# Probabilities turned on VectorE, a later landing in the order, other care for VectorE, and an untied end, in a fused attention and expert kernel

## The chip, the cores and the metric

One core of one Trainium2 chip. The time is the device time of one execution in microseconds (us), the median of several. Beside it stands one profiled execution, from which all rows below are read. Engines: TensorE (PE, matmuls), VectorE (DVE), ScalarE (ACT), GpSimd (POOL), SyncE (SP, here only an issuer of DMA transfers). Each takes its own queue of instructions in order.

## What is computed

```python
q_s = softmax(q, axis=-1); k_s = softmax(k, axis=2)          # 4 x 8 heads, 576 x 64 each
x = q_s @ (k_s.T @ v)                                        # to 2304 tokens x 512
h = x @ w_in                                                 # 512 -> 2048
g = where(h >= 1, h, where(h <= -1, 0, (h + 1)**2 / 4))
x = g @ w_out                                                # 2048 -> 512
p = domain_probs / (domain_probs.sum(-1) + 1e-9)             # 2304 x 4
out = sum(p[:, e] * (relu(x @ w1[e]) @ w2[e]) for e in range(4))   # 512 -> 1024 -> 512
```

Inputs are normal random numbers; the first layer's weights come in double precision, the rest in single.

## The kernel before

The 2304 tokens are cut into five blocks of 512, 512, 512, 256 and 512 (block 0 to 4). `PASSES` puts blocks 1 and 0 into a first pass and blocks 2 and 4, with block 3 as `rest`, into a second. In each pass all first-layer weights are used (kind "a"), then the weights of the four experts (kind "b"). Within a kind the hidden width is taken in chunks of 128 and the chunks in groups, one after the other over the blocks. Every product is made of three matmuls of rounded halves (`products`, L1114 to L1116). Except in the first pass's first layer, a pair of blocks and a pair of chunks are multiplied with seven products in place of eight (`strassen`); in the second pass's experts the second matrix too (`second_pairs`), so that there the pair's results are transposed outputs that have to be combined and turned at the end (`finish_pairs`: `total`, then `turned`), while block 3's come out in rows (`finish_expert`, then a store to `out`).

Around the matmuls the other engines prepare: a weight is loaded into `words`, rounded to its high half by a cast (L479, ScalarE or VectorE) and subtracted for its low half (L484, VectorE or GpSimd). `strassen` needs sums of quarters of the weights (`sums`, also L484). In the first pass's experts these are made once and stored to DRAM (`keep_sums`); in the second they are loaded. First-layer weights are converted once and `kept` in DRAM. Attention of the last two batches (`keys`, `queries`) runs beside the first pass's experts.

No engine's order is written out by hand. `Order.run` plays the kernel forward in Python while it is built: each piece of work is a generator that yields an engine with a duration, a list of engines with durations to choose from, an event, or a number, which is its due time in steps of the order. Among the work that can start earliest, the lowest due time goes first. The instructions are emitted in that order, so durations and due times that the planner holds decide each queue's order; at run time the engines wait on semaphores. Three of its rules matter here:

- `arrival` says when a transfer lands: 128 partitions' bytes at 360 GB/s behind the transfer before, plus a constant of 0.9 us.
- `way` chooses between engines. It takes the earliest end, where an engine's duration is lengthened by its recent load (half-life 40 us), a weight of 6 for VectorE, 1 for ScalarE and 0 for GpSimd, and `order.care`:

```python
weight = 0.0 if isinstance(t.want, Soon) else self.WEIGHT[own] * self.care
end = start + d * (1 + weight * self.busy(own, self.now) / self.SPAN)
```

- `order.care` is 1.0 until the second pass's experts begin, then 0.1 (set in `ups`).

`norm_probs` loads the probabilities into `pn` (128 partitions x 18 token tiles x 4 experts), normalises them on VectorE and stores those of blocks 2 and 4 to DRAM as four rows of 1024 (`rows_of_p`), turned by the store's access pattern. In the second pass's experts `load_p` loads each row, broadcast over all partitions, and `weighted` multiplies with it. `downs` emits the second matrix's matmuls group by group: for each group it yields its due step, the weight, the hidden values, and a PSUM bank of `out_banks`. The last group's order is: `second_pairs` of blocks 2 and 4, then block 3's plain matmuls, then, at due time `len(steps)`, the totals, the transposes and the stores.

Of the kernel before, what the change touches and what calls it, by code (L numbers as in the profile page):

```python
# [17 lines left out]
P = 128  # L18
# [46 lines left out]
class Order:  # L65
# [4 lines left out]


    HOP = 0.2
    SPAN = 40.0
    WEIGHT = {DVE: 6.0, ACT: 1.0, POOL: 0.0, PE: 0.0, SP: 0.0}
    NEAR = 0.05
# [77 lines left out]
    def arrival(self, issued, size):  # L153

        self.dma_free = max(issued + 0.45, self.dma_free) + size * P / 360e3
        return self.dma_free + 0.9

    def rank(self, t, engine):
        return t.due - self.AHEAD.get((t.kind, engine), 0)
# [22 lines left out]
def dve(n):  # L182
    return DVE, 0.14 + n * 0.00107
# [15 lines left out]
def attention_moe_kernel(  # L199
# [46 lines left out]
    LAST = 2  # L246
    LATER = 4
    CARE = 0.1
    GATE_DUE = 1
    groups = []  # L250
    for pair, rest in PASSES:
# [45 lines left out]
    one = const.tile([P, 1], F32, name="one")  # L297
    rebias = const.tile([P, 1], F32, name="rebias")
    pn = const.tile([P, NT // P, NE], F32, name="pn")
    psum_p = const.tile([P, NT // P], F32, name="psum_p")  # L300


# [202 lines left out]
    def norm_probs():  # L505
        start = Event()
        start.set(150.0)
        yield start
        for i in range(NT // P):
            for o, n, rows in token_rows(probs, i * P, P):  # L510
                t = yield SP, 0.65
                nc.sync.dma_start(out=pn[o:o + n, i, :], in_=rows)
        late = Event()
        late.set(t + 3)
        yield late
        t = yield dve(300)
        nc.vector.tensor_reduce(out=psum_p, in_=pn, axis=AX.X, op=ALU.add)
        nc.vector.tensor_scalar(out=psum_p, in0=psum_p, scalar1=EPS, scalar2=None, op0=ALU.add)
        nc.vector.reciprocal(out=psum_p, in_=psum_p)
        nc.vector.tensor_tensor(  # L520
            out=pn, in0=pn, in1=psum_p.unsqueeze(2).to_broadcast([P, NT // P, NE]), op=ALU.mult
        )
        probs_in.set(t)
        i0 = blocks[PASSES[1][0][0]][0] // P
        at = 0
        for bi in PASSES[1][0]:
            b0, n = blocks[bi]
            for i in range(n // P):
                t = yield SP, 0.65
                nc.sync.dma_start(  # L530
                    out=rows_of_p[:, at:at + P].rearrange("e p -> p e"), in_=pn[:, b0 // P + i, :]
                )
                at += P
        rows_in.set(t + 5)


# [700 lines left out]
    def ups():  # L1237
        for s, (g, j) in enumerate(steps):
            bi, ws = groups[g]
            w = used(g, j)  # L1240
            t0, n = blocks[bi]
            if w[0] == "b" or is_kept(w):
                i, kind = w[3], w[0]
                pair, rest = PASSES[i]
                if bi == pair[0] and j % 2 == 0:

                    ahead = 4 if kind == "a" and g == order_of[bi, kind][-1] else 0
                    yield s - ahead
                    if g + 3 * len(PASSES[i]) >= order_of[bi, kind][-1] and i + 1 < len(PASSES):
                        if near[i + 1].time is None:  # L1250
                            near[i + 1].set(order.running.time)
                    if g > order_of[0, "b"][0] and calm.time is None:
                        calm.set(order.running.time)
                    if kind == "b" and i:
                        order.care = CARE
                    yield from strassen(i, g, j)
                    if rest is not None:
                        for k in range(2):
                            yield from plain_rest(i, g + 2, j + k)
                    t = order.running.time  # L1260
                    for x in slot_of.pop((w, 0)):
                        units.put(x, t)
                continue
            yield s
            bank = yield ups_banks
            gate = ((yield gates), (yield gates))
            yield ready[w, 0]
            ah, al = first_of(w)
            for c in range(KC):
                for event in of_block(bi, c):  # L1270
                    yield event
                t = yield pe(n, 3)
                products(
                    bank[:, :n], ah[:, c, :], al[:, c, :], xh[bi][c], xl[bi][c],
                    c == 0, c == KC - 1,
                )
            order.add(gated(g, j, bank[:, :n], n, lambda t, bank=bank: ups_banks.put(bank, t),
                            gate=gate), "ffn")
            if s == last_a[bi]:
                for x in xparts[bi]:  # L1280
                    xfree.put(x, t)
# [245 lines left out]
    def gated(g, j, h, n, give, in_psum=True, gate=None):  # L1527
# [28 lines left out]
        gate_of[g, j] = gate, gh, gl  # L1556
        hidden[g, j].set(t + MARGIN)

    def downs():
        s0 = 0  # L1560
        for g, (bi, ws) in enumerate(groups):
            n, kind, nj = blocks[bi][1], ws[0][0], len(ws)
            if is_paired(used(g, 0)) and bi in PASSES[used(g, 0)[3]][0]:
                if bi == PASSES[used(g, 0)[3]][0][0]:
                    for j in range(0, nj, 2):
                        yield s0 + j
                        yield from second_pairs(g, j)
                s0 += nj
                continue
            m = KC if kind == "a" else n // P  # L1570
            place = order_of[bi, kind]
            each = [(j, c) for j in range(nj) for c in range(m)]
            if kind == "a" and bi == PASSES[0][0][1] and g == place[-1]:

                each = [x for x in each if x[0] < 2] + [(j, c) for c in CORDER for j in range(2, nj)]
            ps, left, begun = {}, [m] * nj, [0] * m
            for j, c in each:
                w = used(g, j)
                if left[j] == m:
                    yield s0 + j  # L1580
                    yield ready[w, 1]
                    yield hidden[g, j]
                _, gh, gl = gate_of[g, j]
                bh, bl = second_of(w)
                first, last = begun[c] == 0, begun[c] == nj - 1
                begun[c] += 1
                if first:
                    ps[c] = yield out_banks[c]
                cs = slice(c * P, (c + 1) * P)
                t = yield pe(n if kind == "a" else DM, 3)  # L1590
                if kind == "a":
                    products(ps[c][:, :n], bh[:, cs], bl[:, cs], gh, gl, first, last)
                else:
                    products(ps[c], gh[:, cs], gl[:, cs], bh, bl, first, last)
                if last:
                    order.add((finish_first if kind == "a" else finish_expert)(
                        bi, w, c, ps[c], g == place[0], g == place[-1]), "ffn")
                left[j] -= 1
                if not left[j]:
                    for x in gate_of.pop((g, j))[0]:  # L1600
                        give_gate(x, t)
                    if step_of[w][1] == s0 + j:
                        x = slot_of.pop(w)
                        for x in x if isinstance(x, tuple) else (x,):
                            units.put(x, t)
            s0 += nj

    SECOND = (("A11", "B11"), ("S4", "B22"), ("A12", "B21"), ("S1", "T1"), ("S3", "T3"),
# [64 lines left out]
    def finish_pairs():  # L1673
# [31 lines left out]
            temps.put(dst, t + 3)  # L1705

        for c in range(2):
            order.add(total(c), "ffn", len(steps))
        for bi, which in ((b2, (1, 3)), (b1, (0, 2))):
            for k in range(blocks[bi][1] // P):  # L1710
                yield made[0][which[0]]
                bank = yield ups_banks
                for d in range(KC):
                    i, c = which[d // 2], d % 2
                    yield made[c][i]
                    src = pairs_out[2 + 2 * i + c]
                    yield pe(P, 2)
                    nc.tensor.transpose(
                        bank[:, d * P:(d + 1) * P], src[:, k * P:(k + 1) * P], ident
                    )  # L1720
                order.add(turned(bi, k, bank), "ffn", len(steps))

    def finish_first(bi, w, c, p, first, last):
        n = blocks[bi][1]
        if first:
            yield acc_free[bi]
# [4 lines left out]
        else:  # L1731
            t = yield dve(n)
            nc.vector.tensor_tensor(out=dst, in0=p[:, :n], in1=dst, op=ALU.add)  # L1733
        out_banks[c].put(p, t)
        if last:
            y_in[bi, c].set(t)

    def finish_expert(bi, w, c, p, first, last):
        i = blocks[bi][0] // P + c
        dst = acc[bi][:, c * DM:(c + 1) * DM]  # L1740
        yield probs_in
# [6 lines left out]
        else:  # L1748
            nc.vector.scalar_tensor_tensor(  # L1749
                out=dst, in0=p, scalar=by, in1=dst, op0=ALU.mult, op1=ALU.add  # L1750
            )
        out_banks[c].put(p, t)
        if last:
            for o, m, rows in token_rows(out, i * P, P):
                t = yield SP, 0.5
# [8 lines left out]
    with tc.manual_schedule():  # L1764
# [15 lines left out]
        order.add(ups(), "ffn")  # L1780
        order.add(prepare_all(), "ffn")
        order.add(gate_operands(), "ffn")
        order.add(finish_pairs(), "ffn", len(steps))
        order.add(load_p(), "load")
        order.add(norm_probs(), "load", len(steps))
        order.add(keep_warm(), "warm", 10 * len(steps))
# [33 lines left out]
```

## Time and profile before

| | |
|---|---|
| median of 3 runs | 1262.95 us (1262.72 to 1267.39) |
| profiled execution, its own time | 1272.47 us |
| its span, first to last instruction | 1270.7 us |
| mean granted TensorE clock | 0.984 of full speed |
| busy TensorE / VectorE / ScalarE / GpSimd | 1219.2 / 820.0 / 519.8 / 730.2 us |

Matmuls are pipelined: the timeline gives each a duration of about 0.39 us while the next starts 0.227 us later, so busy time counts them as overlapping. An idle time is put down to the instruction or transfer that came last among those waited for. Windows are given in us from the span's start. The first pass's first layer ends at about 250 us, its experts at 610, the second pass's first layer at 860.

### The profile page before, as it was taken

Reading aid. Unit: us, or ns where it says so; the run is one execution under the profiler, and the core shown is the slowest. Engines: PE = TensorE matmul, PEld = TensorE weight load, DVE = VectorE, ACT = ScalarE, POOL = GpSimd, SP = SyncE. Lnnn points to the kernel's source line nnn. Section 1 sums busy time; section 2 is a strip of 40 time slices with the busy share of each in tenths; the row PEclk is TensorE's granted clock in tenths of the full one; section 3 lists DMA queues with packets and bytes.
Section 4 is the critical chain, followed back from the end, with each engine's and each line's share of the span. In section 5 each row is a group of like instructions: output and inputs, shape, how many; then the busy total and the mean of one; then the engine's idle time right before and its main releaser. Section 6 shows DMA issues by size and latency. Waiting matters only on the chain.

```text
span 1270.7 us, 16472 instructions
## 1 busy us (share of the span) xinstructions
PE 1219.2 (96%) x5802; PEld 1006.3 (79%) x5802; DVE 820.0 (65%) x1246; ACT 519.8 (41%) x957; POOL 730.2 (57%) x680
## 2 busy tenths in 40 slices
PE   9989999599999999999999999999999999999996
PEld 6868888467878778888788888887888888888885
DVE  5977783366655665444651735658777787787786
ACT  4667654343544434332454433625232232233221
POOL 2413231648788878776666737423675576566652
PEclk9989999799999999999999999999999999999999
DMA  8656659316556543534283221513234433443312
GB/s 230 197 176 241 200 200 50 127 41 199 170 191 198 169 157 127 179 126 144 70 258 102 68 86 48 166 51 130 103 133 145 137 133 116 148 135 110 115 42 83
DMA packets 109458, 174.67 MB, mean 137 GB/s; under 512 B 34880, under 2 KB 67648, under 8 KB 109376
## 3 DMA queue, kind: packets, MB, share of 16 engines
q1 hardware_dynamic: 108576, 172.31, 44.6%
q10 hardware_dynamic: 800, 1.31, 0.3%
q8 instruction: 46, 0.75, 0.3%
q14 instruction: 36, 0.29, 0.1%
HBM read 118.53 MB, written 55.07 MB: 137 GB/s over the span
## 4 chain that ended last, share of the span: by engine, by line
PE 82%; DVE 6%; DMA 5%; ACT 2%; issue 2%; POOL 1%; SPq 1%; ACTq 0%; DVEq 0%; POOLq 0%
PE bank L1115 26%; PE bank L1114 26%; PE bank L1116 26%; DMA rows_of_p<-pn 1%; DMA words<-in_moe_w_dram 1%; PE bank L975 1%; PE bank L1070 1%; DVE x L484 1%; PE bank L1109 1%; PE bank L1060 1%; DVE gate_late L484 1%; POOL w L484 1%; DMA w<-kept 1%; DMA acc<-in_k_dram 0%; DVE mk L914 0%
## 5 line engine op out<-in xcount | busy, mean ns | idle before, releaser
L1114 PE MATMUL bank<-x,w 128*128 128x512 f32 (+1 forms) x988 | 373.5, 378 | 21.5 <-DVE cv L1545 12.4
L1115 PE MATMUL bank<-x,w 128*128 128x512 f32 (+1 forms) x988 | 368.0, 372 | 5.6 <-DVE x L484 3.5
L1116 PE MATMUL bank<-x,w 128*128 128x512 f32 (+1 forms) x988 | 366.8, 371 | 0.0
L1114 PEld LDWEIGHTS bank<-x,w 128*128 128x128 f32 x988 | 187.4, 190 | 60.9 <-DVE cv L1545 13.3
L1115 PEld LDWEIGHTS bank<-x,w 128*128 128x128 f32 x988 | 187.7, 190 | 39.9 <-DVE x L484 6.0
L1116 PEld LDWEIGHTS bank<-x,w 128*128 128x128 f32 x988 | 187.5, 190 | 31.9
L484 POOL TENSOR_TENSOR w<-words,w 128x512 fp32r<-128x512 f32 (+1 forms) x112 | 137.2, 1237 | 89.8 <-ACT w L479 58.3
L1666 DVE TENSOR_TENSOR acc<-bank,acc 128x512 f32<-128x512 f32 x182 | 120.0, 686 | 23.2 <-PE bank L1116 23.2
L484 POOL TENSOR_TENSOR gate_late<-cv,gate_late 128x512 fp32r<-128x512 f32 (+1 forms) x68 | 88.5, 1309 | 75.2 <-ACT gate_late L479 74.8
L484 POOL TENSOR_TENSOR w<-cv,w 128x512 fp32r<-128x512 f32 x75 | 97.7, 1306 | 33.7 <-ACT w L479 31.6
L484 POOL TENSOR_TENSOR x<-cv,x 128x512 fp32r<-128x512 f32 x29 | 42.8, 1476 | 108.8 <-ACT x L479 91.9
L1114 PE MATMUL bank<-w,gate 128*128 128x512 f32 x240 | 98.3, 410 | 0.0
L479 ACT CAST gate_late<-cv 128x512 fp32r<-128x512 f32 (+1 forms) x80 | 47.8, 601 | 120.6 <-DVE cv L1441 86.3
L1115 PE MATMUL bank<-gate_late,w 128*128 128x512 f32 (+1 forms) x248 | 94.7, 382 | 2.1 <-DVE gate_late L484 1.8
L1114 PE MATMUL bank<-gate_late,w 128*128 128x512 f32 (+1 forms) x248 | 94.1, 379 | 2.1 <-DVE acc L1733 2.1
L1116 PE MATMUL bank<-w,gate 128*128 128x512 f32 x240 | 94.5, 394 | 0.0
L1115 PE MATMUL bank<-w,gate 128*128 128x512 f32 x240 | 94.4, 393 | 0.0
L1116 PE MATMUL bank<-gate_late,w 128*128 128x512 f32 (+1 forms) x248 | 93.8, 378 | 0.0
L479 ACT CAST w<-words 128x512 fp32r<-128x512 f32 (+1 forms) x120 | 68.4, 591 | 54.2 <-DMA words<-in_moe_w_dram 30.0
L1749 DVE SCALAR_TENSOR_TENSOR acc<-bank,pn,acc 128x512 f32<-128x512 f32 x70 | 49.4, 749 | 52.2 <-PE bank L1116 52.2
L484 POOL TENSOR_TENSOR gate<-cv,gate 128x512 fp32r<-128x512 f32 (+1 forms) x44 | 53.8, 1228 | 47.9 <-ACT gate L479 47.9
L1115 PE MATMUL bank<-gate,w 128*128 128x512 f32 (+1 forms) x188 | 70.4, 375 | 2.9 <-POOL gate L484 2.8
(227 smaller groups left out, 2303.3 us busy)
## 6 DMA issues: line engine op xcount, KB each, us to landing
words<-in_moe_w_dram SPq DMA_DIRECT2D x64, 512.0 KB, 4.3
sums<-w SPq DMA_DIRECT2D x64, 512.0 KB, 4.9
w<-sums SPq DMA_DIRECT2D x64, 512.0 KB, 4.5
kept<-w SPq DMA_DIRECT2D x32, 512.0 KB, 4.9
w<-kept SPq DMA_DIRECT2D x32, 512.0 KB, 4.3
words<-in_moe_w_in_dram SPq DMA_DIRECT2D x16, 512.0 KB, 4.7
words<-in_moe_w_out_dram SPq DMA_DIRECT2D x16, 512.0 KB, 6.0
wide<-in_k_dram SPq DMA_DIRECT2D x20, 160.0 KB, 5.4
```

Source lines behind the costliest of these rows:

```text
L479: nc.scalar.copy(out=dst, in_=src)
L484: (nc.vector if engine == DVE else nc.gpsimd).tensor_tensor(**kw)
L975: nc.tensor.matmul(bank[:, :N], ek[:, c, :], vt_buf[:, c * N:(c + 1) * N], start=(c == 0), stop=(c == NC - 1),)
L1060: nc.tensor.transpose(bank[:, i * P:i * P + m], eq[:m, c], ident[:m, :m])
L1070: nc.tensor.matmul(bank[:, :hi - lo], bd, qt_buf[:, lo:hi], start=True, stop=True)
L1109: nc.tensor.matmul(bank[:, :P], ident, ident, start=True, stop=True)
L1114: nc.tensor.matmul(ps, al, bh, start=first, stop=False, **kw)
L1115: nc.tensor.matmul(ps, ah, bl, start=False, stop=False, **kw)
L1116: nc.tensor.matmul(ps, ah, bh, start=False, stop=last, **kw)
L1666: nc.vector.tensor_tensor(out=dst, in0=p, in1=dst, op=ALU.add)
L1749: nc.vector.scalar_tensor_tensor(out=dst, in0=p, scalar=by, in1=dst, op0=ALU.mult, op1=ALU.add)
```

## The change

Four things change. `norm_probs` copies the probabilities of blocks 2 and 4 into 32 columns, turns them in 32x32 blocks on VectorE and stores them with four transfers whose runs are 32 numbers long, in place of eight transfers that turn element by element. `arrival`'s constant goes from 0.9 to 1.9 us. `order.care` is 0.15 in the first pass's experts, 1 in the second pass's first layer, and 0.1 in its experts as before. At the end, the body of `downs` becomes `group_downs`; the last group's matmuls (block 3) are handed to a task of their own, with a due time 8 steps later and with banks of `ups_banks`, and the totals and transposes are due 8 steps earlier.

```diff
+    LANDING = 1.9
...
-        return self.dma_free + 0.9
+        return self.dma_free + self.LANDING
...
+    CARE1 = 0.15
+    CARE2 = 1
+    END = 8
+    REST_LATER = 8
...
+    p_cols = const.tile([P, 32], F32, name="p_cols")
+    p_rows = const.tile([P, 32], F32, name="p_rows")
...
-        i0 = blocks[PASSES[1][0][0]][0] // P
-        at = 0
-        for bi in PASSES[1][0]:
-            b0, n = blocks[bi]
-            for i in range(n // P):
-                t = yield SP, 0.65
-                nc.sync.dma_start(
-                    out=rows_of_p[:, at:at + P].rearrange("e p -> p e"), in_=pn[:, b0 // P + i, :]
-                )
-                at += P
+        yield dve(100)
+        for k, bi in enumerate(PASSES[1][0]):
+            i0, m = blocks[bi][0] // P, blocks[bi][1] // P
+            nc.vector.tensor_copy(
+                out=p_cols[:, k * m * NE:(k + 1) * m * NE].rearrange("p (i e) -> p i e", e=NE),
+                in_=pn[:, i0:i0 + m, :],
+            )
+        yield dve(64)
+        nc.vector.transpose(out=p_rows, in_=p_cols)
+        for r in range(P // 32):
+            t = yield SP, 0.65
+            nc.sync.dma_start(
+                out=rows_of_p.rearrange("e (i r j) -> i e r j", r=P // 32, j=32)[:, :, r],
+                in_=p_rows[r * 32:(r + 1) * 32],
+            )
...
-                    if kind == "b" and i:
-                        order.care = CARE
+                    order.care = {("b", 0): CARE1, ("a", 1): CARE2, ("b", 1): CARE}[kind, i]
...
+    def group_downs(g, s0, banks=None, later=0):
...
+                yield s0 + j + later
...
+                ps[c] = yield (out_banks[c] if banks is None else banks)
...
+            if g == len(groups) - 3:
+                order.add(group_downs(g + 2, s0 + 2 * nj, ups_banks, REST_LATER), "ffn",
+                          s0 + 2 * nj + REST_LATER)
...
+            if g < len(groups) - 1:
+                yield from group_downs(g, s0)
...
-            order.add(total(c), "ffn", len(steps))
+            order.add(total(c), "ffn", len(steps) - END)
...
-                order.add(turned(bi, k, bank), "ffn", len(steps))
+                order.add(turned(bi, k, bank), "ffn", len(steps) - END)
...
-        order.add(finish_pairs(), "ffn", len(steps))
+        order.add(finish_pairs(), "ffn", len(steps) - END)
```

## Rows read from the trace of the kernel before

**Rows 1.** The page, part 1: busy us (share of the span) xinstructions
```profile
PE 1219.2 (96%) x5802; PEld 1006.3 (79%) x5802; DVE 820.0 (65%) x1246; ACT 519.8 (41%) x957; POOL 730.2 (57%) x680
```

**Rows 2.** TensorE's waits over the whole span: us in total, times, longest
```profile
PE bank L1114 <- DVE cv L1545: 12.4, 1, 12.4
```

**Rows 3.** Timeline of TensorE, 192 to 246 us: start, duration [idle before <-what ended it]
```profile
221.93 0.39 PE L1116 MATMUL bank<-x,w 128*128 128x512 f32 x1
234.76 0.79 PE L1114 MATMUL bank<-x,w 128*128 128x512 f32 x1 [12.44 <-DVE cv L1545]
...
237.24 0.80 PE L1114 MATMUL bank<-x,w 128*128 128x512 f32 x1 [0.83 <-ACT x L479]
...
239.75 0.80 PE L1115 MATMUL bank<-x,w 128*128 128x512 f32 x1 [1.72 <-POOL x L484]
...
244.61 0.40 PE L1114 MATMUL bank<-gate,w 128*128 128x512 f32 x1
```

**Rows 4.** Stretches: length, busy PE, PEld, DVE, ACT, POOL; granted clock, DMA share, GB/s
```profile
204.00:208.00 4.00, 4.00 (x19) 3.31 (x18) 1.10 (x2) 2.65 (x5) 1.73 (x2) 1.00 2.62 0
232.00:236.00 4.00, 1.24 (x3) 0.83 (x3) 1.29 (x2) 1.76 (x3) 4.00 (x6) 0.50 0.13 54
```

**Rows 5.** Timeline of ScalarE, 192 to 246 us
```profile
228.75 0.62 ACT L479 CAST w<-words 128x512 fp32r<-128x512 f32 x1 [21.25 <-DMA words<-in_moe_w_dram]
```

**Rows 6.** Timeline of SyncE's DMA queue, 192 to 246 us
```profile
194.38 4.45 SPq L530 DMA_DIRECT2D rows_of_p<-pn  x8
211.29 0.81 SPq L828 DMA_DIRECT2D kept<-w  x2
212.15 9.17 SPq L606 DMA_DIRECT2D words<-in_moe_w_dram  x3
```

**Rows 7.** DMA issues of the whole kernel: KB each, median us to landing
```profile
words<-in_moe_w_dram SPq DMA_DIRECT2D x64, 512.0 KB, 4.3
...
pn<-in_moe_domain_probs_dram SPq DMA_DIRECT2D x36, 1.0 KB, 3.1
...
rows_of_p<-pn SPq DMA_DIRECT2D x8, 2.0 KB, 26.5
```

**Rows 8.** Timeline of VectorE, the same subtraction twice, 1222 to 1250 us
```profile
1223.03 1.50 DVE L484 TENSOR_TENSOR gate<-cv,gate 128x512 fp32r<-128x512 f32 x1
...
1248.66 0.68 DVE L484 TENSOR_TENSOR gate<-cv,gate 128x512 fp32r<-128x512 f32 x1
```

**Rows 9.** Timeline of VectorE, 192 to 246 us
```profile
201.01 1.28 DVE L818 SCALAR_TENSOR_TENSOR w<-x,t 128x1024 fp32r<-128x1024 f32 x1
...
216.99 0.69 DVE L1539 TENSOR_SCALAR cv<-bank 128x512 f32<-128x512 f32 x1 [10.20 <-PE bank L1116]
```

**Rows 10.** One stretch, the experts' first pass: columns as in rows 4
```profile
250.00:610.00 360.00, 352.82 (x1580) 284.53 (x1579) 206.84 (x318) 146.72 (x287) 267.81 (x279) 1.00 0.47 152
```

**Rows 11.** GpSimd's costliest group in 250 to 610 us: busy, mean ns | idle before
```profile
L484 POOL TENSOR_TENSOR w<-cv,w 128x512 fp32r<-128x512 f32 x58 | 75.4, 1305 | 24.2 <-ACT w L479 22.1 <-issue 1.9
```

**Rows 12.** Timeline of TensorE, 460 to 470 us
```profile
468.86 0.50 PE L1114 MATMUL bank<-x,w 128*128 128x512 f32 x1 [2.37 <-DVE gate L1513]
```

**Rows 13.** Timeline of VectorE, 460 to 470 us
```profile
463.99 1.27 DVE L914 TENSOR_TENSOR mk<-wide 128x128 f32<-128x128 f32 x1
```

**Rows 14.** Timeline of TensorE, 666 to 670 us
```profile
669.28 0.50 PE L1115 MATMUL bank<-gate,w 128*128 128x512 f32 x1 [2.75 <-POOL gate L484]
```

**Rows 15.** Timeline of TensorE, 1240 to 1262 us
```profile
1252.15 0.40 PE L1114 MATMUL bank<-w,gate 128*128 128x512 f32 x1
...
1257.62 2.78 PE L1718 MATMUL bank<-ident,acc 128*128 128x128 f32 x24
```

**Rows 16.** Timeline of VectorE, 1240 to 1262 us
```profile
1253.45 3.38 DVE L484 TENSOR_TENSOR acc<-acc,acc 128x512 f32<-128x512 f32 x4
```

**Rows 17.** One stretch at the end: columns as in rows 4
```profile
1260.00:1270.00 10.00, 1.50 (x12) 1.02 (x10) 1.64 (x3) 1.75 (x3) 0.00 (x0) 0.76 0.82 243
```

**Rows 18.** One stretch, the experts' second pass: columns as in rows 4
```profile
860.00:1240.00 380.00, 377.00 (x1817) 315.31 (x1816) 296.29 (x450) 117.63 (x215) 238.85 (x181) 1.00 0.36 121
```

More of the change, by code (lines that the diff above doesn't have):

```diff
@@ L1557, in gated @@
         hidden[g, j].set(t + MARGIN)
+    def group_downs(g, s0, banks=None, later=0):
+        bi, ws = groups[g]
+        n, kind, nj = blocks[bi][1], ws[0][0], len(ws)
+        m = KC if kind == "a" else n // P
+        place = order_of[bi, kind]
+        each = [(j, c) for j in range(nj) for c in range(m)]
+        if kind == "a" and bi == PASSES[0][0][1] and g == place[-1]:
+            each = [x for x in each if x[0] < 2] + [(j, c) for c in CORDER for j in range(2, nj)]
+        ps, left, begun = {}, [m] * nj, [0] * m
+        for j, c in each:
+            w = used(g, j)
+            if left[j] == m:
+                yield s0 + j + later
+                yield ready[w, 1]
+                yield hidden[g, j]
+            _, gh, gl = gate_of[g, j]
+            bh, bl = second_of(w)
+            first, last = begun[c] == 0, begun[c] == nj - 1
+            begun[c] += 1
+            if first:
+                ps[c] = yield (out_banks[c] if banks is None else banks)
+            cs = slice(c * P, (c + 1) * P)
+            t = yield pe(n if kind == "a" else DM, 3)
+            if kind == "a":
+                products(ps[c][:, :n], bh[:, cs], bl[:, cs], gh, gl, first, last)
+            else:
+                products(ps[c], gh[:, cs], gl[:, cs], bh, bl, first, last)
+            if last:
+                order.add((finish_first if kind == "a" else finish_expert)(
+                    bi, w, c, ps[c], g == place[0], g == place[-1],
+                out_banks[c] if banks is None else banks), "ffn")
+            left[j] -= 1
+            if not left[j]:
+                for x in gate_of.pop((g, j))[0]:
+                    give_gate(x, t)
+                if step_of[w][1] == s0 + j:
+                    x = slot_of.pop(w)
+                    for x in x if isinstance(x, tuple) else (x,):
+                        units.put(x, t)
     def downs():
@@ L1561, in downs @@
         for g, (bi, ws) in enumerate(groups):
-            n, kind, nj = blocks[bi][1], ws[0][0], len(ws)
+            nj = len(ws)
+            if g == len(groups) - 3:
+                order.add(group_downs(g + 2, s0 + 2 * nj, ups_banks, REST_LATER), "ffn",
+                          s0 + 2 * nj + REST_LATER)
             if is_paired(used(g, 0)) and bi in PASSES[used(g, 0)[3]][0]:
@@ L1569, in downs @@
                 continue
[L1570 to L1605, printed above, removed]
+            if g < len(groups) - 1:
+                yield from group_downs(g, s0)
             s0 += nj
@@ L1720, in finish_pairs, with finish_first @@
                     )
-                order.add(turned(bi, k, bank), "ffn", len(steps))
-    def finish_first(bi, w, c, p, first, last):
+                order.add(turned(bi, k, bank), "ffn", len(steps) - END)
+    def finish_first(bi, w, c, p, first, last, banks):
         n = blocks[bi][1]
@@ L1733, in finish_first, with finish_expert @@
             nc.vector.tensor_tensor(out=dst, in0=p[:, :n], in1=dst, op=ALU.add)
-        out_banks[c].put(p, t)
+        banks.put(p, t)
         if last:
             y_in[bi, c].set(t)
-    def finish_expert(bi, w, c, p, first, last):
+    def finish_expert(bi, w, c, p, first, last, banks):
         i = blocks[bi][0] // P + c
@@ L1751, in finish_expert @@
             )
-        out_banks[c].put(p, t)
+        banks.put(p, t)
         if last:
```

## The prediction

> **What bounds the kernel now.** I read the page's shares first, then TensorE's waits, then the timeline around the longest of them. TensorE is busy 96% of the span [rows 1]. Its matmuls of 512 columns start every 0.227 us at full clock, and nothing in the diff removes one, so the change can only take away idle time, at most 1270.7 - 1219.2 = 51.5 us, and the slow matmuls that follow long idle times. The waits put one idle time far above the rest: 12.4 us at a matmul of L1114 [rows 2]. The reader should follow that one back.
>
> In TensorE's timeline [rows 3] the last first-layer matmul starts at 221.93 us and the next at 234.76; two more gaps of 0.83 and 1.72 follow. In 232 to 236 us the granted clock is 0.50, which is 1.2 GHz [rows 4]; the matmuls behind the gap run at that level until 244.61. The engine named, VectorE, is only the last link. On ScalarE a cast of weights (`w`, L479) starts at 228.75 after 21.25 us idle, and what ended the wait is the transfer of `words` [rows 5]; ScalarE and VectorE take their queues in order, so the gate work that TensorE wanted stood behind that cast. On SyncE's queue the eight transfers `rows_of_p<-pn` (L530) are issued from 194.38 on, the next transfer only at 211.29, and the `words` loads from 212.15 [rows 6]. They land 26.5 us after issue, the median [rows 7]. In 204 to 208 us the DMA engines are shown as fully taken while 0 GB/s are moved [rows 4]: 8 x 128 x 4 = 4096 separate four-byte runs, scattered over DRAM. Once they drain, the weights arrive, 16 us late.
>
> **The scatter (norm_probs).** Removed: 8 transfers, 4096 runs. Added: two VectorE copies of 128x16, one 32x32 block transpose, 4 transfers of 32 runs of 128 bytes, all behind the same normalisation. The VectorE work is three small instructions; none of that kind is shown. Below stands nothing, above three times the 0.68 us of a whole 512-wide operation [rows 8], 2 us; I take 0.7 us, nearer to small operations, and it hides, since VectorE has 10 us with nothing to do before 217 us [rows 9]. SyncE waits behind the transpose as it waited behind the normalisation; the transfers queued behind it, `kept` and `words`, need data that is ready only when the conversion's last VectorE operation ends at 201.01 + 1.28 = 202.29 us [rows 9]. For the four transfers the nearest rows lie on both sides: if each run costs what a four-byte run did (4096 in about 28 us, from the first issue at 194.38 until the drain near 222), 128 runs cost 0.9 us; the loads of the probabilities, in 16-byte runs, land after 3.1 us [rows 7]. Either way they are gone by 200 us.
>
> Then the `words` loads go out near 203 us. At the 4.3 us that this load takes over the whole kernel [rows 7] they land near 208, 20 us earlier than 228.75. The chain from that cast to the matmul took 234.76 - 228.75 = 6.0 us, so its data is ready near 214, and the two smaller gaps' near 219, all before TensorE asks at 222.16. The 15 matmuls up to 244.61 then take 15 x 0.227 = 3.4 us from 222.16 on, to 225.6. Saved: 244.6 - 225.6 = **19.0 us**, of it 15.0 idle and 4.0 slow clock and issue. Lower bound: the profiled execution took 1272.5 us against a median of 1262.95, an excess of 9.5 us, and a drain of tiny DMA runs is the likeliest place for a profile to cost time; if the whole excess sits there, a timed run gains 19.0 - 9.5 = 9.5 us.
>
> **More to VectorE in the experts' first pass.** The planner lengthens VectorE's duration by 6 x care x load / 40, where load is its recent busy time with a half-life of 40 us (57.7 times its share). At the share of 206.84 / 360 [rows 10] load is 33; a 512-wide subtraction that it puts at 0.76 us counts as 4.6 us at care 1 and as 1.3 us at 0.15, against 1.31 us of GpSimd. So it was almost never VectorE, and is now a toss-up decided by who is free. GpSimd was busy 267.81 of 360 us [rows 10], 75.4 of them on 58 such subtractions at 1305 ns [rows 11]. I estimate that a third to a half of GpSimd's work moves, putting some 45 us on VectorE at half the price, and its share goes from 57 to about 70%. What TensorE can gain is the stretch's idle 360 - 352.82 = 7.2 us plus about 1.6 us of slow clock behind the longest wait. What it can lose: that wait, 2.37 us at 468.86, is already VectorE's; three max operations of the attention (L914, one of 1.27 us for 128 columns) ran ahead of a gate operation [rows 12, 13]. With its slow clock it costs 4.0 us. Bounds: -8.8 to +8 us (two more such waits). I take **-1 us**, since the GpSimd waits that go are about as many as the VectorE waits that may come.
>
> One thing speaks against the exchange rate. The same 512-wide subtraction takes 0.68 us on VectorE, but 1.50 us when GpSimd is running one [rows 8]. The Trainium skill, SBUF — State Buffer, "SBUF: two separate sides", says that a VectorE operation with two SBUF inputs and a GpSimd operation that reads SBUF take a shared port pair as an exclusive lock for a whole instruction; the two rows agree. By its rule the moved work would cost VectorE up to 1.50 / 0.68 = 2.2 times as much, some 95 us instead of 45, and a share of 84%; that is the last rival below.
>
> **Longer transfers in the order (LANDING).** The planner's 512 KB load went from 3.5 to 4.5 us after issue, and 4.3 were measured [rows 7]. It changes only which instruction stands ahead of which. Where it can pay is the one remaining wait that a load causes: 2.75 us at 669.28, at GpSimd's subtraction queued behind `w<-kept` [rows 14]; but those loads come in a burst, where each waits for the one before, and one microsecond may not cover that. Bounds -2.75 to +1, taken **-1 us**. In the first 90 us order changes can fall either way; I take zero.
>
> **The end.** The last `rest` group's 24 second-layer matmuls run from 1252.15 to 1257.6, after the last pair product and before the transposes [rows 15]. They no longer stand in that line: totals and transposes are due earlier, and these matmuls fill what is free, in other banks. VectorE's four totals end at 1256.83 [rows 16], but the last two serve the second block; the two that the first transposes need are done near 1255.2. So the transposes can start 2.4 us earlier. From there the end is output: in 1260 to 1270 us the DMA engines are 82% busy at 243 GB/s [rows 17], and the bytes stay. Bounds 0 to -4; taken **-2 us**.
>
> **The sum.** -19 - 1 - 1 - 2 = -23 us: 1272.5 goes to 1249.5 in a profile. How it stands to the median is open: if the 9.5 us of excess stay, timed runs take 1240; if the stall takes them with it, 1249.5. The predicted time lies between, **1244 us**.
>
> **The rivals.**
> - The wait moves. With the load early, GpSimd's preparation of the experts' weights may end last at the same seam, as it worked through it once the loads came. For it: in 232 to 236 us GpSimd was busy without a break [rows 4]. Against: it stood idle while the loads were late, and has that time now. 6 us back: 1250.
> - The stall is mostly the profile's: all the excess sits in the drain, and the small terms come to nothing: 1262.95 - 9.5 = 1253.
> - The change doesn't do what it says: 128-byte runs clog as before. Against: 128 runs for 4096; even half the delay would end before 222 us. The time would be about 1261.
> - Slower: VectorE becomes the bound in the first pass. There are eight attention units in it; if each makes one wait like that at 468.86, 8 x 4.0 - 4.0 = 28 us come back: 1244 + 28 = 1272. It decides from about six such waits on. For it: the 1.50 us row and the wait itself. Against: in the second pass the same engine is at three quarters and TensorE hardly waits [rows 18].
>
> **How the numbers follow.** Forecast 0.78 (1238 to 1250), moved wait 0.09, profile's stall 0.08, slower 0.03, no effect 0.02. The range reaches from a clean sum with the pass's waits halved, 1234, to the profile's stall, 1253. Half a percent, 6.3 us, is about what a measurement tells from no change: faster needs under 1256.6. The first three cases are faster, less a little for mishaps that add up: 0.94; same 0.03; slower 0.03.
>
> **What would show it.** Right: the four transfers land in about 3 us; `words` lands near 208 us; no idle above 2 us on TensorE between 215 and 245 us, and the clock stays at 1.00; GpSimd under 200 of 360 us in the first pass; transposes start before the last `rest` matmul. Wrong: a new wait of several microseconds before 250 us; VectorE named in many waits between 250 and 610 us, each with a clock drop behind it; or a profile that improves by 23 us while the timed runs improve by 10.

## The result and the profile after

The changed kernel takes 1245.45 us, the median of 4 runs (1244.27 to 1248.04), against 1265.17 us for the one before (4 runs, the three of the table above and one more): a ratio of 0.9846, 95% interval 0.9815 to 0.9878, or 19.5 us less (15.4 to 23.4). The profiled execution fell from 1272.47 to 1244.38 us, its span from 1270.7 to 1242.6.

To say where the time went, this table counts progress. All kernels here issue the same 5232 product matmuls. For each kernel the products in the timeline of TensorE were added up by their columns in order of start, and the time at which a given share had started was compared with the profile of before. A number is how much later (+) or earlier (-) in us the kernel reached that point. 12% lies before the seam between the first layer and the experts, 14% behind it; 44% is the end of the first pass's experts; 46% lies behind the seam to the second pass; 50% behind the wait at the kept weights [rows 14]; 98% before the end.

```
kernel                               12%     14%     44%     46%     50%     98%   last
changed kernel                      +1.4   -17.7   -20.5   -23.7   -26.8   -26.4  -28.5
e1   store alone                    -1.1   -20.2   -20.1   -21.7   -24.7   -24.8  -24.9
e2   landing alone                  +3.5    -5.6    -7.5    -8.9   -11.8   -13.6  -13.6
e3   care alone                     +1.0    -2.1    -7.1   -10.3    -9.5   -10.6  -10.6
e4   end alone                      +0.1    -5.9    -5.9    -7.4    -6.8    -6.8   -8.9
e5   all but landing                -0.9   -19.9   -25.2   -28.4   -29.8   -28.9  -31.0
e6   all but care                   +5.9   -13.2   -15.1   -14.8   -17.8   -17.7  -19.8
e7   all but the end                +4.8   -14.2   -15.6   -18.8   -21.9   -23.1  -23.1
e8   scatter from ScalarE's queue   -1.4    -5.7    -7.0    -8.5    -7.8    -7.9   -7.9
e9   scatter in 16-byte runs        +0.4   -18.7   -20.1   -20.2   -20.7   -20.8  -20.8
e10  landing late only at the start +4.3   -14.8   -20.2   -23.4   -22.5   -22.0  -24.1
e11  landing late only behind 500   +0.4   -18.7   -23.8   -26.8   -29.9   -29.9  -32.1
e12  changed kernel again           +5.2   -13.8   -16.8   -19.9   -23.0   -22.6  -24.8
```

The first row reads: the start lost 1.4 us; the seam gave 19.1; the first pass's experts 2.8; the seam behind them 3.2; the wait at the kept weights 3.1; the rest until the end lost 0.4; the end gave 2.1, and 0.4 were lost in the output behind the last product. Together 28.1, the difference of the spans. The last row is the same kernel in another execution: it stands 3.8 us later at 12%, and from there on no step differs by more than 0.3 us. So the start of a single row says little.

**The seam.** SyncE's queue in the changed kernel, where [rows 6] stood before, then the DMA packets between 197.5 and 200 us, then the first weight cast on ScalarE [rows 5]:

```profile
196.34 2.89 SPq L542 DMA_DIRECT2D rows_of_p<-p_rows  x4
202.75 1.31 SPq L840 DMA_DIRECT2D kept<-w  x2
204.11 2.90 SPq L618 DMA_DIRECT2D words<-in_moe_w_dram  x3
```

```profile
DMA packets 160, 0.02 MB, mean 7 GB/s; under 512 B 160, under 2 KB 160, under 8 KB 160
```

```profile
210.35 0.62 ACT L486 CAST w<-words 128x512 fp32r<-128x512 f32 x1 [1.44 <-DMA words<-in_moe_w_dram]
```

The four stores are issued in 2.9 us. The profile has no landing time for them, but the sizes in the trace's DMA records show their 128 packets of 128 bytes, all between 197.72 and 199.97 us, so the data had been moved 3.6 us after the first issue; the `words` loads leave at 204.11, not 212.15, and the cast starts at 210.35, not 228.75. VectorE's three small instructions:

```profile
195.81 0.25 DVE L534 COPY p_cols<-pn 128x16 f32<-128x16 f32 x2
196.10 0.21 DVE L539 STREAM_TRANSPOSE p_rows<-p_cols 128x32 f32<-128x32 f32 x1
```

They take 0.46 us; the prediction took 0.7, with bounds of 0 and 2. TensorE has no wait over 0.2 us between 126 and 250 us. Four stretches of the changed kernel (columns as in rows 4): two of the seam, then the first pass's experts as in [rows 10], then the output:

```profile
204.00:208.00 4.00, 4.00 (x20) 3.30 (x19) 1.18 (x2) 3.41 (x6) 2.16 (x2) 1.00 0.82 287
232.00:236.00 4.00, 4.00 (x19) 3.34 (x18) 2.84 (x3) 0.55 (x1) 1.52 (x2) 1.00 0.01 4
230.00:590.00 360.00, 353.39 (x1593) 285.92 (x1592) 224.12 (x348) 144.14 (x278) 258.59 (x268) 1.00 0.46 152
1232.00:1242.00 10.00, 2.34 (x20) 1.87 (x18) 2.31 (x4) 1.76 (x3) 0.00 (x0) 0.71 0.81 233
```

The DMA engines move 287 GB/s in 204 to 208 us where they moved nothing, and the clock is 1.00 where it was 0.50. TensorE's waits over the whole span, then how often and the longest:

```profile
PE bank L987 <- DVE w L830: 3.8, 1, 3.8
PE bank L1127 <- DVE x L491: 3.4, 5, 1.4
PE bank L1126 <- DVE acc L1755: 2.1, 1, 2.1
PE bank L1126 <- POOL w L491: 1.9, 2, 1.1
PE bank L929 <- DVE mk L926: 1.9, 1, 1.9
```

The 12.4 us at the head of the list are gone, and so are the 2.4 us of [rows 12] and the 2.75 us of [rows 14]. The list now begins with 3.8 us at L987, a matmul of the attention at 82 us; its counterpart before, at 81 us, had no wait. That row is the one to follow up.

**The end.** TensorE, then VectorE:

```profile
1226.71 0.39 PE L1128 MATMUL bank<-w,gate_late 128*128 128x512 f32 x1
1226.94 0.27 PE L1740 MATMUL bank<-ident,acc 128*128 128x128 f32 x1
1226.97 0.47 PE L1126 MATMUL bank<-w,gate_late 128*128 128x512 f32 x1
...
1230.73 2.51 PE L1740 MATMUL bank<-ident,acc 128*128 128x128 f32 x21 [1.23 <-DVE acc L491]
```

```profile
1228.63 1.45 DVE L1771 SCALAR_TENSOR_TENSOR acc<-bank,pn,acc 128x512 f32<-128x512 f32 x2 [0.23 <-PE bank L1128]
1230.00 1.28 DVE L491 TENSOR_TENSOR acc<-acc,acc 128x512 f32<-128x512 f32 x2
```

The first transpose (L1740) starts at 1226.94, before the last `rest` matmuls, as was forecast. But most of them wait 1.23 us until 1230.73 for the totals on VectorE, which had the two `rest` results (L1771, 1.45 us) ahead of the last two totals. The output then runs at 233 GB/s, with the DMA engines 81% busy, about as before [rows 17].

### The profile page after: what moved, and what is told of

Read it like the earlier page. It is cut to its first block, busy times and chain, and to the rows that moved or that the text cites. A ratio compares the mean times of both kernels' runs of the same rounds, so it can differ in the third digit from the quotient of the medians.

```text
span 1242.6 us, 16505 instructions
## 1 busy us (share of the span) xinstructions
PE 1211.1 (97%) x5816; PEld 1003.9 (81%) x5816; DVE 833.8 (67%) x1270; ACT 517.2 (42%) x949; POOL 723.5 (58%) x669
## 4 chain that ended last, share of the span: by engine, by line
PE 87%; DVE 7%; DMA 2%; ACT 1%; issue 1%; POOL 1%; SPq 0%; ACTq 0%; POOLq 0%; DVEq 0%
PE bank L1127 28%; PE bank L1126 27%; PE bank L1128 27%; PE bank L987 2%; DVE x L491 1%; PE bank L1082 1%; PE bank L1121 1%; PE bank L1072 1%; DVE gate L1524 1%; DVE gate_late L491 1%; DMA words<-in_moe_w_out_dram 1%; DVE acc L1771 1%; DMA words<-in_moe_w_in_dram 0%; DMA acc<-in_v_dram 0%; DVE acc L491 0%
## 5 line engine op out<-in xcount | busy, mean ns | idle before, releaser
L491 POOL TENSOR_TENSOR w<-words,w 128x512 fp32r<-128x512 f32 (+1 forms) x108 | 133.2, 1247 | 78.5 <-ACT w L486 50.6
L491 POOL TENSOR_TENSOR gate_late<-cv,gate_late 128x512 fp32r<-128x512 f32 (+1 forms) x64 | 83.3, 1305 | 65.3 <-ACT gate_late L486 63.5
L491 POOL TENSOR_TENSOR w<-cv,w 128x512 fp32r<-128x512 f32 x69 | 91.0, 1323 | 44.8 <-ACT w L486 41.1
L491 POOL TENSOR_TENSOR x<-cv,x 128x512 fp32r<-128x512 f32 x29 | 44.8, 1545 | 98.7 <-ACT x L486 72.1
L491 POOL TENSOR_TENSOR gate<-cv,gate 128x512 fp32r<-128x512 f32 (+1 forms) x48 | 61.0, 1272 | 58.5 <-ACT gate L486 58.5
L486 ACT CAST gate_late<-cv 128x512 fp32r<-128x512 f32 (+1 forms) x75 | 44.8, 599 | 102.9 <-DVE cv L1452 74.2
L1771 DVE SCALAR_TENSOR_TENSOR acc<-bank,pn,acc 128x512 f32<-128x512 f32 x70 | 49.5, 750 | 37.1 <-PE bank L1128 37.1
```

The costliest lines, as they stand in the source:

```text
L486: nc.scalar.copy(out=dst, in_=src)
L491: (nc.vector if engine == DVE else nc.gpsimd).tensor_tensor(**kw)
L1771: nc.vector.scalar_tensor_tensor(out=dst, in0=p, scalar=by, in1=dst, op0=ALU.mult, op1=ALU.add)
```

## The experiments

All times are medians against the kernel before on the same chip.

**e1, the store alone, in the kernel before** (the other three parts left as they were).

```diff
-                t = yield SP, 0.65        # eight four-byte scatters
-                nc.sync.dma_start(out=rows_of_p[:, at:at + P].rearrange("e p -> p e"), ...
+        nc.vector.transpose(out=p_rows, in_=p_cols)   # and four stores of 128-byte runs
```

> The kernel before with the transposed store alone (copies, block transpose, four transfers of 128-byte runs). Theory A, the parts add up: the profile's seam at 222 us closes and its span falls by 19 us, with nothing after it changed; a timed run gains 10 to 14 us, since the profile of before exceeds the timed runs by 7 us and the one of after does not. Rival B, the drain is as long without a profile: a timed run gains 18 to 20 us and the other three parts together nothing. Rival C, the wait moves when this part is made alone, with the loads still planned too early: under 8 us in either.

Measured: 1247.81 us against 1265.16 (29 runs), ratio 0.9866 (0.9842 to 0.9889): 17.3 us of the 19.7 between the medians of before and of the changed kernel. So the store is most of the change, and the gain lies between theory A's 10 to 14 us and rival B's 18 to 20. In the profile the seam gave 19.1 us, as theory A had it, but the whole span fell by 25.3. "Nothing after it changed" was wrong: 4.6 us more came between 44% and 50%, at the seam behind the first pass's experts and at the kept weights. The planned order doesn't explain these, since apart from the store all queues of e1 hold the same instructions in the same order as before. The profile of before, at 1272.47, lies above all 29 runs (1259.89 to 1270.22) and 7.3 us above their median. The profile of e1 lies 0.6 below its own, and 25.3 less these two is the 17.3 measured.

**e4, the end alone**, whose order until 1240 us is that of before (the diff's `group_downs`, `END` and `REST_LATER`).

> The kernel before with the untied end alone (last group in a task of its own with other banks, totals and transposes due 8 steps earlier). Theory A: the same order until about 1220 us, then the profile's end comes 2 us earlier; timed 1 to 3 us faster. Rival B, output transfers alone set the end: no change within 0.5 us in the stretch behind the last product.

Measured: 1263.21 us, ratio 0.9980 (0.9963 to 0.9997), and 2.1 us behind 98% in the table. Theory A before the last product; behind it the output took 0.8 us longer. e4 also shows a second execution of the same scatter, in the same order of all queues. SyncE's queue and TensorE's wait at the seam:

```profile
194.54 5.52 SPq L535 DMA_DIRECT2D rows_of_p<-pn  x8
207.78 0.81 SPq L833 DMA_DIRECT2D kept<-w  x2
208.64 7.01 SPq L611 DMA_DIRECT2D words<-in_moe_w_dram  x2
```

```profile
229.55 0.80 PE L1119 MATMUL bank<-x,w 128*128 128x512 f32 x1 [7.08 <-DVE cv L1549]
```

The loads leave 14.1 us after the first store, where it was 17.8, and TensorE waits 7.1 us, where it was 12.4. Measured against a kernel without the scatter the seam costs 19.1 us in the profile of before and 13.1 here, with 16.0 in e3 and 10.0 in e2: the drain's length changes from execution to execution. The DMA records of the traces go with it: between 193 and 235 us a four-byte packet took 84, 82, 60 and 58 ns on average in before, e3, e4 and e2. (In e8 below the stores are issued over 28 us, among moving data, and don't compare.) The 6.0 us between before and e4 are the likely part of the excess of 9.5 us that the prediction could not place. Timed runs have no trace, so the length of the drain in them is not shown.

**e8, the scatter from ScalarE's queue, and e9, the scatter in longer runs**, both in the kernel before.

```diff
-                t = yield SP, 0.65
-                nc.sync.dma_start(
+                t = yield ACT, 0.65
+                nc.scalar.dma_start(
```

> The kernel before with the eight four-byte stores issued from ScalarE's queue in place of SyncE's. Theory A, the runs occupy the DMA engines whatever queue they come from: the weights' loads wait nearly as long, the stall in front of the experts stays at 5 us or more, timed within 5 us of before. Rival B, what counts is standing behind them in the same queue: the loads on SyncE's queue land within 8 us of issue, the stall is under 2 us, and a timed run gains 10 us or more.

```diff
                 nc.sync.dma_start(
-                    out=rows_of_p[:, at:at + P].rearrange("e p -> p e"), in_=pn[:, b0 // P + i, :]
+                    out=rows_of_p.rearrange("f (i p e) -> (f i) p e", i=2, e=NE)[at // P],
+                    in_=pn[:, b0 // P + i, :],
```

> The kernel before with the same eight stores from the same place, but each partition's four probabilities stored as one run of 16 bytes in place of four runs of 4 bytes; the rows are not turned, so the second pass's experts are weighted with the wrong probabilities. Theory A, the drain goes by the number of runs: a quarter of them, landing 5 to 9 us after issue, the stall in front of the experts gone, timed 15 to 18 us faster than before, as with the transposed store. Rival B, any short run to DRAM costs by the transfer: landing still about 20 us, the stall stays, within 5 us of before.

Measured: e8 1266.75 us, ratio 1.0001 (0.9979 to 1.0023); e9 1248.98 us, ratio 0.9861 (0.9825 to 0.9898). The DMA issues of e8 between 200 and 230 us (KB each, median us to landing), then SyncE's queue in e9 and the landing of its stores:

```profile
words<-in_moe_w_dram SPq DMA_DIRECT2D x3, 512.0 KB, 16.9
...
rows_of_p<-pn ACTq DMA_DIRECT2D x7, 2.0 KB, 17.6
```

```profile
194.78 3.67 SPq L530 DMA_DIRECT2D rows_of_p<-pn  x8
201.72 1.30 SPq L829 DMA_DIRECT2D kept<-w  x2
203.08 2.27 SPq L607 DMA_DIRECT2D words<-in_moe_w_dram  x3
```

```profile
rows_of_p<-pn SPq DMA_DIRECT2D x8, 2.0 KB, 2.0
```

Theory A in e8. The weights' loads stand in another queue than the scatter, and still land 16.9 us after issue, against 4.3 over the whole kernel [rows 7]; TensorE waits 8.4 us at the seam. What the runs take is the DMA engines, not a place in a queue. The Trainium skill says so (Trainium Kernel Development and Optimization, Key Constraints): transfers of all issuing queues run on the same 16 engines; e8 agrees.

In e9 the stores have the same place, number and bytes, and a quarter of the runs; they land after 2.0 us and the seam costs nothing, as with the transposed store. Theory A in the main, though the drain is shorter than its quarter (5 to 9 us). The Trainium skill, DMA: Bandwidth & Descriptors, Specifications, puts the boundary at 512 bytes, below which an engine reads, modifies and writes. Here 128-byte and 16-byte runs both lie under it; the first were gone 3.6 us after their first issue, the second landed after 2.0 us; of the three sizes only the four-byte runs, 4096 of them, were slow. A rival stays untested: e9 changes the length of a run, the number of runs and their place, since its runs lie side by side in DRAM where the four-byte ones are scattered. Which of the three matters is not shown.

**e2 and e3, the landing and the care alone**, in the kernel before.

```diff
-        return self.dma_free + 0.9
+        return self.dma_free + 1.9
```

> The kernel before with the later landing alone (1.9 in place of 0.9 us). Theory A: the scatter stall stays; the idle time at the subtraction behind the kept weights (2.75 us at 669 us) goes, and with the one at the start of the second pass's first layer (2.27 us and its slow clock) 6 us less in the profile from 600 us on; 1 to 2 us more before 130 us; timed 3 to 6 us faster. Rival B, those two stalls went because of the care: this kernel keeps both, and is 0 to 2 us slower.

```diff
-                    if kind == "b" and i:
-                        order.care = CARE
+                    order.care = {("b", 0): 0.15, ("a", 1): 1, ("b", 1): CARE}[kind, i]
```

> The kernel before with the other care alone (0.15 in the first pass's experts). Theory A: 1 to 3 us less between 250 and 610 us, GpSimd's busy time there falls by 5 us and VectorE's rises by 20 as in the changed kernel, nothing else moves; timed 0 to 3 us faster, within noise. Rival B: it also takes the two stalls behind 610 us, 6 us more, timed 6 to 9 us faster. Rival C, more VectorE work makes new waits when the load is planned early: slower by 2 us or more.

Measured: e2 1263.34 us, ratio 0.9992 (0.9973 to 1.0011), no difference that can be told; e3 1260.18 us, ratio 0.9966 (0.9948 to 0.9983). In the table care gains 5.0 us in the first pass's experts and 3.2 at the seam behind them, and loses 0.8 at the kept weights; the landing gains 2.9 at the kept weights, but the start is 3.5 later. So each theory had half. The wait at the seam is the care's. The wait at the kept weights goes in all six kernels that are planned with the later landing there, but it varies by itself too: of the eight without, seven keep 1.6 to 2.8 us, and e1 none, in the order of before. And the scatter's stall, which changes by itself, stood in both.

**e5, e6, e7: the changed kernel with one part put back**, where the scatter no longer blurs them (`LANDING = 0.9`; `CARE1 = 1`; the old end).

> The changed kernel with the planner's landing put back to 0.9 us. Theory A, with the scatter gone the later landing is worth nothing and costs at the start: both kernels planned with it stand 1.4 us later after 6% of the products, where both planned without stand 0 to 1 us earlier or level; so 1 to 3 us faster than the changed kernel, 1242.5 to 1244.5. Rival B, it removes the wait at the kept weights here too: that wait comes back, and this kernel takes 1247 to 1249.

> The changed kernel with care put back to 1 in the first pass's experts (VectorE weighed as heavily as before). Theory A, the care is worth what it was worth alone, 4 us: 1249 to 1250, with the VectorE waits between 250 and 610 us and the 2.3 us wait at the start of the second pass's first layer back. Rival B, with the weights loaded on time GpSimd keeps up and the care is worth nothing: 1245 to 1246.

> The changed kernel with the old end (last group in line behind the pair products, totals and transposes due at the last step). Theory A: 2 us more, all behind the last pair product; 1247 to 1248. Rival B: the output transfers set the end, 1245 to 1246.

Measured: e5 1239.40 us, ratio 0.9782 (0.9757 to 0.9808); e6 1250.08, ratio 0.9871 (0.9851 to 0.9892); e7 1248.48, ratio 0.9844 (0.9820 to 0.9868). Without the later landing the kernel is faster than with it, by more than theory A had. The care is worth 3 to 5 us: without it TensorE's wait at the second pass is back, with half a clock for some matmuls behind it. First that wait in e6 and its stretch; then the same wait in the changed kernel; then the wait at the kept weights, which e5 has and the changed kernel has not:

```profile
605.09 0.50 PE L1126 MATMUL bank<-x,w 128*128 128x512 f32 x1 [2.53 <-DVE cv L1374]
```

```profile
605.00:615.00 10.00, 9.91 (x36) 8.01 (x37) 6.63 (x11) 3.91 (x7) 5.16 (x6) 0.83 0.18 40
```

```profile
597.79 0.50 PE L1126 MATMUL bank<-x,w 128*128 128x512 f32 x1 [0.67 <-DVE cv L1374]
```

```profile
639.55 0.50 PE L1127 MATMUL bank<-gate_late,w 128*128 128x512 f32 x1 [1.59 <-POOL gate_late L491]
```

The end can't be told from nothing by e7's timed runs; the table shows 2.1 to 2.2 us between 98% and the last product in every kernel that has it and none in every one that has not. Behind the last product these kernels lose 0.4 to 0.8 us of it in the output.

**e10, e11, e12: where the later landing loses**, on one chip with the changed kernel itself.

```diff
-        return self.dma_free + self.LANDING
+        return self.dma_free + (self.LANDING if issued < 150.0 else 0.9)     # e10
+        return self.dma_free + (self.LANDING if issued > 500.0 else 0.9)     # e11
```

> The changed kernel with the later landing only for transfers issued before 150 us in the plan, 0.9 us behind that. Theory A, the landing's loss is made in the attention at the start: the kernel stands 2 to 6 us later after 12% of the products than without it, and takes 1242 to 1245. Rival B, the loss is made in the experts' first pass, where it also reorders: 1238 to 1241.

> The changed kernel with the later landing only for transfers issued behind 500 us in the plan. Theory A: the start is as without it, the wait at the kept weights goes, 1 to 2 us faster than with 0.9 throughout: 1237 to 1239, the fastest of all. Rival B, the wait moves to the next load: 1239 to 1241.

> The changed kernel itself, beside the other kernels of this call on one chip. Theory A: 1244 to 1247, 4 to 7 us above the kernel with the landing only late. Rival B, the 6 us between it and the kernel without the later landing came from two chips: under 2 us.

Measured: e10 1245.63 us, ratio 0.9840 (0.9812 to 0.9869); e11 1238.93, ratio 0.9793 (0.9766 to 0.9821); e12 1246.96, ratio 0.9855 (0.9827 to 0.9882). Theory A's mechanism each time, though e10 is 0.6 us over its range and the 8.0 us between e12 and e11 are 1 more than its 7. e11 has the lowest median of all, and is not to be told from e5.

The mechanism stands in the queues at the start. VectorE, the keys' subtractions (`bank` in, 640 wide, L491), in e12 and then in e11:

```profile
69.11 1.76 DVE L813 TENSOR_SCALAR words<-words 128x1024 int32<-128x1024 int32 x1
...
71.13 0.81 DVE L491 TENSOR_TENSOR acc<-acc,bank 128x640 f32<-128x640 f32 x1
71.86 1.21 DVE L815 SCALAR_TENSOR_TENSOR x<-words 128x1024 fp32r<-128x1024 uint32 x1
...
76.67 0.81 DVE L491 TENSOR_TENSOR wide<-acc,bank 128x640 f32<-128x640 f32 x1
```

```profile
65.75 0.76 DVE L491 TENSOR_TENSOR acc<-acc,bank 128x640 f32<-128x640 f32 x1
...
68.09 0.69 DVE L813 TENSOR_SCALAR words<-words 128x1024 int32<-128x1024 int32 x1
...
72.04 0.81 DVE L491 TENSOR_TENSOR wide<-wide,bank 128x640 f32<-128x640 f32 x1
```

SyncE, the loads of V into the buffers that these subtractions have read, in e12 and then in e11:

```profile
71.96 2.54 SPq L976 DMA_DIRECT2D acc<-in_v_dram  x4
...
77.52 4.24 SPq L976 DMA_DIRECT2D acc<-in_v_dram  x4
```

```profile
66.54 2.53 SPq L976 DMA_DIRECT2D acc<-in_v_dram  x4
...
73.18 1.21 SPq L976 DMA_DIRECT2D wide<-in_v_dram  x2
```

TensorE, the last product of keys and values of the start, in e12 and then in e11:

```profile
85.93 2.22 PE L987 MATMUL bank<-acc,wide 128*128 128x130 f32 x10 [3.87 <-POOL wide L981]
```

```profile
81.50 1.29 PE L987 MATMUL bank<-wide,wide 128*128 128x130 f32 x10
```

Told that loads land 1 us later, the planner puts other work of VectorE ahead of the subtractions. In e12 the step L813 of the first weights' conversion stands ahead of the first one, in e11 behind it; ahead of the second e12 has the whole rest of that conversion (until L830), e11 only as far as L819. VectorE then reaches the subtractions 5.4 and 4.6 us later. The loads of V can't start before, since they write the same buffer: they start 5.4 and 4.3 us later, and the product waits 3.87 us and starts 4.4 later. Until there e12 was not behind: at 1% of the products it stands 2.6 us earlier than e11, at 1.5% it stands 2.8 later. The six kernels with the later landing at the start share this wait (3.4 to 3.9 us) and one of 1.2 us near 129 us, for converted weights; the others have neither. A constant that was nearer to the median landing made the order worse, because a whole chain (subtract, load, product) hung on it.

## Why the prediction was right

**The seam** was read rightly down to the number: 19.0 us forecast, 19.1 in the profile, `words` landed at about 210 us against 208. It holds in each of the nine profiles without four-byte runs. But 19.0 is the size of one long drain: other profiles paid 10 to 16 us for the same stores. The prediction laid the excess of 9.5 us on the profile; e4 and e3 show that the drain varies by itself, and that the profile of before had caught a long one. In timed runs e1 and e9 gained 17.3 and 15.7 us in all, between the two ends that the prediction named; how much of that is the seam is not shown.

**The experts' first pass** was taken at -1 us and gave -2.8. The size of the cause was off: I estimated that 45 us of work go to VectorE; between 230 and 590 us it took 17 us more than in [rows 10], and GpSimd 9 less. The sign named for it, GpSimd under 200 us, did not come: it was 258.59. Why the planner moved so little was not followed. So neither the slower rival nor the 84% of the port's rule (45 x 2.2 is 99 us, so 85%) was put to the test: VectorE's share is 62%. A term was missing: the wait at the seam to the second pass, 2.3 us, went to 0.67 us with the care (e6 brings it back). That gave 3.2 us, of which 1.6 are a slow clock that follows this wait in before but not in e1, e2, e4 and e8.

**The landing** is the step that failed. The wait at the kept weights went, 3.1 us in the profile where I took 1 and bounded it by 2.75; e5 keeps 1.6 us of it, though e1 lost it without the later landing. But "in the first 90 us order changes can fall either way; I take zero" was wrong: the six kernels planned with the later landing at the start stand 4.2 us later at 12%, the mean of +1.4 to +5.9, the others -0.2 (-1.4 to +1.0, before itself at 0). And it takes back most of the care's gain in the first pass: care gives 5.0 to 5.4 us there without it (e3, e5, e10, e11) and 1.4 to 3.0 with it (changed kernel, e7, e12). The waits show where: the five kernels planned with it in that pass (these three, e2 and e6) have one of 1.8 to 1.9 us at 292 to 304 us, the L929 row of the list above, where TensorE waits for a maximum of the attention on VectorE, and one of 0.7 to 0.8 us near 440; no other kernel has them. In timed runs the part costs about 6 to 8 us, not -1.

**The end** gave 2.1 us in the profile, as taken, less 0.4 in the output, with the transposes starting before the last `rest` matmul; of the 2.4 us that they might have started earlier, 1.23 went to the wait for the last totals.

The predicted 1244 us is 1.5 from the median because the errors cancel: the landing's loss ate what the care gave beyond its estimate. And 1244 was put between 1240 and 1249.5 without a row that decides between them. That it came so near is luck; that the stall at the seam would go is not.

**The rivals.** The wait did not move: nothing in front of 250 us took its place. The stall was not mostly the profile's. The stores do what they say. VectorE did not become the bound.

## What to carry to other kernels

Look at the DMA engines' busy share beside the bytes they move: full and nothing moved was the sign of tiny runs here, and what waits for them can stand in another queue (e8). Turn the data on an engine first, or leave a longer run; here even 16 bytes were enough. When a planner writes the order, a constant that is truer on average can still lose: change it where a trace shows the wait that it is to cure, and measure each part with the others in place.

## What the runs showed of the hardware

4096 stores of four bytes held up the other transfers of a core. In before the DMA engines moved 0 GB/s between 200 and 211 us; the packets of these stores had all started by 211.4, but they landed only at 224.5, and until 224 the loads behind them moved slowly, at 47 GB/s. Why is open. In the 4 us behind that the engines moved 307 GB/s. The slow stretch of before, columns as in rows 4:

```profile
212.00:224.00 12.00, 10.32 (x46) 8.22 (x44) 0.69 (x1) 0.00 (x0) 0.00 (x0) 1.00 1.04 47
```

The stores cost TensorE 10 to 19 us in five profiles (about 15 in e8). The timed runs of before reach over 10.3 us (29 runs), those of the kernels without these stores over 3.1 to 7.7 (4 to 6 runs each), so the spread alone does not show that the drain varies; the profiles do. 1024 stores of 16 bytes in the same eight transfers cost nothing that could be seen.

The same wait was not always followed by a slow clock. Behind 2.3 to 2.5 us at the start of the second pass the granted clock was 0.50 for 3.4 us in before, e6 and e9, and stayed at 1.00 in e1, e2, e4 and e8. The 15 us around it in before, then in e1:

```profile
617.00:632.00 15.00, 12.73 (x49) 10.05 (x49) 9.55 (x13) 5.45 (x9) 9.73 (x10) 0.89 0.20 44
597.00:612.00 15.00, 12.73 (x57) 10.21 (x56) 9.32 (x13) 5.60 (x9) 11.24 (x11) 1.00 0.27 63
```
